# Fetching the first DFT piece over GpSimd's queue, behind a memset of half of its place

## The chip, the cores and the metric

The kernel runs on one core of a Trainium2 chip. The metric is the device time of one execution in microseconds, with all inputs and the output in the chip's memory. The kernel before was timed in three runs: median 867.17 us, lowest 867.04, highest 867.76.

## What is computed

`x` is 2048 tokens by 640 channels, in fp32. After a layer norm over the channels, two branches are added to `x`: the real part of a two-dimensional Fourier transform, written as matrix products, and an MLP that mixes the tokens.

```
x  = A_x
xn = layernorm(x)                                  # over the 640 channels
a  = xn @ dft_hid_re.T ;  b = xn @ dft_hid_im.T
A  = dft_seq_re @ a - dft_seq_im @ b               # 2048 x 2048 times 2048 x 640
u  = gelu(xn.T @ w1 + b1)                          # 640 x 1728
B  = (u @ w2 + b2).T                               # 2048 x 640
out = x + A + B
```

## The kernel before

All products are made in fp32 precision out of reduced-precision parts: an operand is cut into a high part (`high`, line 138, on ScalarE, ACT) and a low part (`low`, line 141, on VectorE, DVE), and each product is three matmuls: high by high, high by low, low by high. The kernel also saves products by sums of blocks (a Strassen-like scheme), which does not touch the place of the change. Work runs in this order: the DFT over the sequence, on columns of the DFT matrices (lines 462 to 659), the DFT over the channels, and the two products of the MLP. The instruction order of every engine is written out by hand (`manual_schedule`).

The change lies in the head, the first some 33 us. `first_columns` (line 462) makes the first 512 columns of both sequence DFT products out of the first four blocks of 128 rows of `x`. Before it, line 135 issues 13 matmuls on a constant (`WARM`), whose result is not used. The string `START` (line 44) gives the order in which the head is issued, a letter for an operation and a digit for its block:

- `x k` (line 513) loads block k of `x`, 128x640 fp32, over SP's queue. Block 0 comes as two halves of 160 KB (line 516), the others whole, 320 KB (line 518).
- `b i` (`load`, line 468) loads piece i of a DFT matrix, 128x512 fp32, 256 KB, into one of the eight places of `raw`, over SP's queue (line 470). `FIRST` (line 36) says which matrix and which block of rows; piece 0 is block 0 of the real matrix.
- `M`, `R`, `F` are the moments of a block (DVE, lines 240 and 246), the inverse root of its variance (DVE line 252, then GpSimd, called POOL in the profile, line 253), and the offset. For block 0 the offset is made by two small instructions on ACT (lines 533 and 537).
- `H` writes the high part of the normalized block (line 377 on DVE for block 0, in a part of 256 columns and one of 384; line 273 on ACT for the others), `N` normalizes the block in place (line 273, ACT), `l` and `L` write its low part (line 141, DVE).
- `T i` and `B i` cut piece i into its high part (line 138, ACT) and its low part (line 141, DVE).
- `P i` issues the matmuls of step i (line 481). The block's columns are the stationary operand, the cut piece is the moving one. The 15 of step 0 are five times high by high, five times high by low, five times low by high. Step 1 has nine, steps 2 to 4 have 15, 9 and 15.

The head's loads are issued in the order `x0 b0 x1 b1 b2 x2 b3 x3 b4 x4 x5 b5 x6 x7 b6 b7`, all on SP. GpSimd's queue carries in the head the memset of line 131, the inverse roots of line 253, and from `C` on (line 458) the stores of finished columns to `y_part`. ACT runs `T0`, the two small instructions of block 0, `N0`, `T1`, `T2` in that order; DVE runs `M0`, `R0`, `H0`, `B0`, the first half of `M1`, `l0`, `L0`, the rest of `M1`.

Of the kernel before, what the change touches and what calls it, by code (L numbers as in the profile page):

```python
# [26 lines left out]
NC = S // CH  # L27
# [13 lines left out]
FIRST_AT = [0, 1, 2, 3, 4, 5, 6, 7, 1, 3]  # L41
# [33 lines left out]
def fnet_plus_mixer(  # L75
# [30 lines left out]
    nc = tc.nc  # L106
# [30 lines left out]
    def high(hi, src):  # L137
        nc.scalar.activation(hi, src, AF.Copy)  # L138

    def low(lo, src, hi):  # L140
        nc.vector.tensor_sub(lo, src, hi.bitcast(F32))  # L141
# [76 lines left out]
    def cut_piece(source, n):  # L218

        held = {}  # L220
        j = len(steps)

        def top():
            held["piece"] = cut_place(j, n)
            high(held["piece"][:, 0, :n], source())

        def bottom():
            hi, lo = (held["piece"][:, i, :n] for i in range(2))
            low(lo, source(), hi)
            return hi, lo  # L230

        return top, bottom
# [4 lines left out]
    def half_moments(k, row, i):  # L237
        if i == 0:
            begun[k] = small.tile([P, 2, 6], F32, name="st")
        nc.vector.bn_stats(begun[k][:, i, :], row[:, i * H2 : (i + 1) * H2])  # L240

    def moments(k, row):
        for i in range(k in begun, 2):
            half_moments(k, row, i)
        st = begun[k]
        nc.vector.bn_aggr(mv[:, k, :], st.rearrange("p a b -> p (a b)"))

    def root(to, var):

        w = var.shape[-1]  # L250
        v = small.tile([P, NS], F32, name="v")[:, :w]
        (nc.vector if w <= 2 else nc.gpsimd).tensor_scalar_add(v, var, EPS)
        nc.gpsimd.tensor_tensor(to, v, power[:, :w], op=ALU.pow)

    def offset(to, ks):
        nc.vector.scalar_tensor_tensor(to[:, 1, ks], mv[:, ks, 0], -1.0, to[:, 0, ks], op0=ALU.mult, op1=ALU.mult)
# [15 lines left out]
    def normalize(k, row, by, to=None):  # L272
        nc.scalar.activation(
            row if to is None else to, row, AF.Identity, scale=by[:, 0, k : k + 1], bias=by[:, 1, k : k + 1]
        )
# [23 lines left out]
    Q = 256  # L299
# [64 lines left out]
    def first_rows(k, which, n=None):  # L364

        q, row = place_of(k)
        a = fixed[0][q]
        if row == 1 or 0 < k < 4:
            parts = [slice(0, D)]
        elif k == 0:  # L370
            parts = [slice(0, Q), slice(Q, D)]
        else:
            parts = [slice(0, Q), slice(2 * Q, D)]
        for cols in parts[n] if n else parts:
            hi, lo = (whole(a, i, row)[:, cols] for i in range(2))
            if which == 0 and k == 0:
                nc.vector.tensor_scalar(
                    hi, x_in[0][:, cols], mv[:, 0, :1], norm[:, 0, :1], op0=ALU.subtract, op1=ALU.mult
                )
            elif which == 0:  # L380
                normalize(k, x_in[k][:, cols], norm, hi)
            else:
                low(lo, x_in[k][:, cols], hi)

    def channels(k, j):

        q, row = place_of(k)
        return [whole(fixed[0][q], i, row)[:, j * P : (j + 1) * P] for i in range(2)]
# [14 lines left out]
    def later_moments(k):  # L403
        moments(k, later_pair(k % 4)[:, (k - 8) // 4, :])
# [46 lines left out]
    def c_tile():  # L451

        i = c_turn[0] = (c_turn[0] + 1) % 6
        return c_place[i // 3][:, i % 3, :]

    def store_y(h, m, c, j, t):
        if h == 0:
            nc.gpsimd.dma_start(y_part[m][c][:, j, :], t)
        else:
            nc.gpsimd.dma_start(y_part[m][c][:, j, :], t, accum_op=ALU.add)  # L460

    def first_columns():


        raw = pieces[1].rearrange("p a q c -> p (a q) c")
        banks = {}

        def load(i):
            m, k = FIRST[i][:2]
            nc.sync.dma_start(raw[:, FIRST_AT[i], :], dft_seq[m * NC, k])  # L470

        def products(w, m, k, j0, j1):

            for js in (range(j0, min(j1, 3)), range(max(j0, 3), j1)) if m else (range(j0, j1),):
                for n, (rows, cols) in enumerate(((0, 0), (0, 1), (1, 0))):
                    for j in js:
                        late = m == 1 and j >= 3
                        first, last = n == 0 and k == (2 if late else 0), n == 2 and k == (1 if late else 3)
                        if first:
                            banks[m, j] = psum[(5 * m + j) % 8]  # L480
                        nc.tensor.matmul(  # L481
                            banks[m, j], channels(k, j)[rows], w[cols], start=first, stop=last, skip_group_check=True,
                        )

        def read(m, js):
            for j in js:
                c = c_tile()
                nc.scalar.activation(c, banks[m, j], AF.Copy)
                store_y(0, m, 0, j, c)

        kept = keep.tile([P, 2, 2, CH], R32, name="kept", tag="slab6")

        def cut_kept(i, k):
            hi, lo = (kept[:, k, a, :] for a in range(2))

            def bottom():
                low(lo, raw[:, FIRST_AT[i], :], hi)
                return hi, lo

            return lambda: high(hi, raw[:, FIRST_AT[i], :]), bottom  # L500

        for i, (m, k, j0, j1) in enumerate(FIRST):
            if j0:
                piece = lambda: None, lambda k=k: (kept[:, k, 0, :], kept[:, k, 1, :])
            elif m == 1 and k < 2:
                piece = cut_kept(i, k)
            else:
                piece = cut_piece(lambda i=i: raw[:, FIRST_AT[i], :], CH)
            steps.append(piece + (lambda w, at=(m, k, j0, j1): products(w, *at),))
        for j in range(ND):  # L510
            extras[8 + j].append(lambda j=j: read(1, (j,)))

        def row(k):
            if k == 0:
                for cols in (slice(0, H2), slice(H2, D)):
                    nc.sync.dma_start(x_in[0][:, cols], x_rows[0][:, cols])  # L516
            else:
                nc.sync.dma_start(x_in[k], x_rows[k])

        def top(i):  # L520
            steps[i][0]()

        def bottom(i):
            ready[i] = steps[i][1]()

        def run(i):
            steps[i][2](ready.pop(i))

        def rooted(k, to=None):
            ks = slice(k, (to or k) + 1)  # L530
            root(norm[:, 0, ks], mv[:, ks, 1])
            if k == 0:
                nc.scalar.activation(norm[:, 1, :1], mv[:, 0, :1], AF.Copy, scale=-1.0)

        def factored(k, to=None):
            if k == 0:
                nc.scalar.activation(norm[:, 1, :1], norm[:, 1, :1], AF.Copy, scale=norm[:, 0, :1])
                return
            offset(norm, slice(k, (to or k) + 1))

        def normalized(k):
            if k < 5:
                normalize(k, x_in[k], norm)
            else:
                nc.vector.tensor_scalar(
                    x_in[k], x_in[k], mv[:, k, :1], norm[:, 0, k : k + 1], op0=ALU.subtract, op1=ALU.mult
                )

        return {
            "x": row, "b": load, "e": later_load, "T": top, "B": bottom, "P": run,  # L550
            "M": lambda k: moments(k, x_in[k]) if k < 8 else later_moments(k), "R": rooted, "F": factored,
            "H": lambda k: first_rows(k, 0), "N": normalized,
            "L": lambda k: first_rows(k, 1, slice(1, None) if k == 0 else None),
            "l": lambda k: first_rows(k, 1, slice(0, 1)), "m": lambda k: half_moments(k, x_in[k], 0), "C": lambda j, to: read(0, range(j, to + 1)),
        }
# [548 lines left out]
    with tc.manual_schedule():  # L1104
        for word in START.split():
            start[word[0]](*map(int, word[1:].split("-")))
        for i in range(8, len(steps) + 1):
# [3 lines left out]
            elif i >= s_hid:  # L1111
                k = sum(i >= s for s in (s_up, s_up + 7 * NF2, s_down))
# [44 lines left out]
```

## Time and profile before

| | |
|---|---|
| median of three runs | 867.17 us (867.04 to 867.76) |
| the profiled execution | 867.26 us, of which the span is 865.4 us |
| PE busy | 860.5 us, 99% of the span |
| DVE, ACT, POOL busy | 698.8 us (81%), 510.7 us (59%), 142.1 us (16%) |
| PE's granted clock | 9 or more tenths in all 40 slices |
| moved over SP's queue (q1) and GpSimd's queue (q0) | 95.72 MB and 50.83 MB |

A row of a timeline reads: start, time taken, engine, line, operation, tile written <- tiles read, shape, count, and in brackets the idle time before it and what ended it. Times are in us from the start of the span. PE is the matmuls, PEld the loads of stationary operands, SPq the issues of SP. A row of a chain reads: start, time taken, what. A row of DMA issues reads: tiles, issuer, operation, count, size, and the median time from issue to landing.

### The profile page before, as it was taken

The page shows a single profiled execution, that of the slowest core. Times are in us where ns is not written, and L with a number is a line of the kernel's source. Part 1 is how long each engine was busy: PE and PEld are TensorE (multiplying, and loading weights), DVE is VectorE, ACT ScalarE, POOL GpSimd, SP SyncE. Part 2 cuts the span into 40 slices and gives each one's busy share as a digit, 9 for nine tenths or more (in the row PEclk, how much of TensorE's full clock was granted, in tenths as well). Part 3 has the DMA queues.
Part 4 walks back from the last instruction along what each step waited for, and adds up shares of the span by engine and source line. Part 5 has one row for each costly group of instructions (what it writes and reads, how often), then busy time and mean ns, then how long its engine had stood idle before and what let it go on. Part 6 is the DMA issues. An engine that isn't in the chain of part 4 may idle for free.

```text
span 865.4 us, 13841 instructions
## 1 busy us (share of the span) xinstructions
PE 860.5 (99%) x4897; PEld 789.3 (91%) x4897; DVE 698.8 (81%) x1181; ACT 510.7 (59%) x928; POOL 142.1 (16%) x191
## 2 busy tenths in 40 slices
PE   9999999999999999999999999999999999999998
PEld 6888888888888888889999999999999999999998
DVE  7899888856767888677877788898779988997886
ACT  5774576543555555447565556675577765565653
POOL 2311111011021210322100101000122221111211
PEclk9999999999999999999999999999999999999999
DMA  9949254493472655779576757454567797656786
GB/s 332 358 86 341 81 193 196 136 369 49 138 142 37 194 109 150 176 120 185 113 165 177 153 138 202 157 188 142 138 156 188 173 264 170 164 133 134 154 181 132
DMA packets 86036, 147.42 MB, mean 170 GB/s; under 512 B 8496, under 2 KB 35504, under 8 KB 85712
## 3 DMA queue, kind: packets, MB, share of 16 engines
q1 hardware_dynamic: 64992, 95.72, 33.2%
q0 software_dynamic: 20976, 50.83, 31.2%
q8 instruction: 38, 0.62, 0.3%
q14 instruction: 30, 0.25, 0.1%
HBM read 99.47 MB, written 52.30 MB: 175 GB/s over the span
## 4 chain that ended last, share of the span: by engine, by line
PE 99%; DMA 0%; SPq 0%; ACT 0%; DVE 0%; issue 0%
PE psum L150 31%; PE psum L151 31%; PE psum L149 31%; PE psum L481 3%; PE psum L177 2%; DMA pieces<-in_dft_seq 0%; SPq L516 0%; ACT piece L138 0%; DVE pair L859 0%
## 5 line engine op out<-in xcount | busy, mean ns | idle before, releaser
L141 DVE TENSOR_TENSOR piece<-pieces,piece 128x512 fp32r<-128x512 f32 (+4 forms) x492 | 322.5, 659 | 122.7 <-ACT piece L138 118.4
L138 ACT ACTIVATE piece<-pieces 128x512 fp32r<-128x512 f32 (+3 forms) x468 | 292.5, 626 | 207.3 <-PE psum L151 109.5
L149 PE MATMUL psum<-piece,n 128*128 128x512 f32 x540 | 210.1, 389 | 0.0
L150 PE MATMUL psum<-piece,n 128*128 128x512 f32 x540 | 210.1, 389 | 0.0
L151 PE MATMUL psum<-piece,n 128*128 128x512 f32 x540 | 210.1, 389 | 0.0
L151 PEld LDWEIGHTS psum<-piece,n 128*128 128x128 f32 x540 | 101.4, 188 | 21.1
L149 PEld LDWEIGHTS psum<-piece,n 128*128 128x128 f32 x540 | 101.4, 188 | 21.1
L150 PEld LDWEIGHTS psum<-piece,n 128*128 128x128 f32 x540 | 101.4, 188 | 20.9
L144 DVE TENSOR_TENSOR pieces<-pieces 128x512 f32<-128x512 f32 (+3 forms) x142 | 111.9, 788 | 2.6
L149 PE MATMUL psum<-sup,piece 128*128 128x320 f32 x368 | 113.7, 309 | 0.0
L150 PE MATMUL psum<-sup,piece 128*128 128x320 f32 x368 | 113.7, 309 | 0.0
L151 PE MATMUL psum<-sup,piece 128*128 128x320 f32 x368 | 113.7, 309 | 0.0
L149 PE MATMUL psum<-sdown,piece 128*128 128x320 f32 x368 | 113.7, 309 | 0.0
L150 PE MATMUL psum<-sdown,piece 128*128 128x320 f32 x368 | 113.7, 309 | 0.0
L151 PE MATMUL psum<-sdown,piece 128*128 128x320 f32 x368 | 113.7, 309 | 0.0
L151 PE MATMUL psum<-shid,piece 128*128 128x320 f32 x280 | 86.6, 309 | 0.0
L149 PE MATMUL psum<-shid,piece 128*128 128x320 f32 x280 | 86.5, 309 | 0.0
L150 PE MATMUL psum<-shid,piece 128*128 128x320 f32 x280 | 86.5, 309 | 0.0
L863 ACT ACTIVATE pair<-psum 128x320 f32<-128x320 f32 x96 | 41.9, 436 | 57.0 <-PE psum L151 51.6
L460 POOL DMA_DIRECT2D y<-c x47 | 41.1, 938 | 185.5 <-DVE c L643 151.0
L149 PEld LDWEIGHTS psum<-sup,piece 128*128 128x128 f32 x368 | 69.1, 188 | 0.0
L150 PEld LDWEIGHTS psum<-sdown,piece 128*128 128x128 f32 x368 | 69.1, 188 | 0.0
(123 smaller groups left out, 1163.2 us busy)
## 6 DMA issues: line engine op xcount, KB each, us to landing
pieces<-in_dft_seq SPq DMA_DIRECT2D x120, 256.0 KB, 5.1
pieces<-in_w SPq DMA_DIRECT2D x88, 256.0 KB, 3.8
y<-c POOLq DMA_DIRECT2D x87, 256.0 KB, 5.6
out<-pair POOLq DMA_DIRECT2D x38, 320.0 KB, 4.8
pieces<-y SPq DMA_DIRECT2D x32, 320.0 KB, 3.7
pieces<-in_w SPq DMA_DIRECT2D x32, 192.0 KB, 3.0
out<-in_x SPq DMA_DIRECT2D x16, 320.0 KB, 8.5
pair<-in_x SPq DMA_DIRECT2D x14, 320.0 KB, 5.1
```

The costliest lines, as they stand in the source:

```text
L138: nc.scalar.activation(hi, src, AF.Copy)
L141: nc.vector.tensor_sub(lo, src, hi.bitcast(F32))
L144: nc.vector.tensor_sub(to, a, b)
L149: nc.tensor.matmul(psum, wh, mh, start=first, stop=False, skip_group_check=True)
L150: nc.tensor.matmul(psum, wh, ml, start=False, stop=False, skip_group_check=True)
L151: nc.tensor.matmul(psum, wl, mh, start=False, stop=last, skip_group_check=True)
L177: nc.tensor.matmul(psum, w, m[i], start=first and i == 0, stop=last and i == 1, skip_group_check=True)
L460: nc.gpsimd.dma_start(y_part[m][c][:, j, :], t, accum_op=ALU.add)
L481: nc.tensor.matmul(banks[m, j], channels(k, j)[rows], w[cols], start=first, stop=last, skip_group_check=True,)
L863: nc.scalar.activation(c, b, AF.Copy)
```

## The change

In `load`, piece 0 alone is treated otherwise. GpSimd first sets 256 of the 512 columns of its place to zero (`Q` is 256), and then issues the transfer on its own queue. The transfer overwrites what the memset wrote, so it waits for the memset. All other pieces stay on SP, whose list of issues becomes one shorter. No later instruction is changed.

```diff
         def load(i):
             m, k = FIRST[i][:2]
-            nc.sync.dma_start(raw[:, FIRST_AT[i], :], dft_seq[m * NC, k])
+            if i == 0:
+                nc.gpsimd.memset(raw[:, FIRST_AT[i], :Q], 0.0)
+            (nc.sync if i else nc.gpsimd).dma_start(raw[:, FIRST_AT[i], :], dft_seq[m * NC, k])
```

## Rows read from the trace of the kernel before

**Rows 1.** The page's chain of waits: shares of the span by engine.
```profile
PE 99%; DMA 0%; SPq 0%; ACT 0%; DVE 0%; issue 0%
```

**Rows 2.** The chain of waits in order of time, its head and its last piece.
```profile
0.74 0.39 SPq L516
...
1.66 3.60 DMA pieces<-in_dft_seq
5.27 0.64 ACT piece L138
5.96 27.50 PE psum L481 x120
...
862.04 0.49 DVE pair L859
```

**Rows 3.** The timeline of the head on PE, DVE and POOL.
```profile
0.79 4.41 PE L135 MATMUL psum<-const-bfloat16-1.0 128*128 128x512 bf16 x13 [0.79 <-PEq L1146]
3.08 0.89 DVE L240 BATCH_NORM_STATS2 st<-x 128x6 f32<-128x320 f32 x2 [3.08 <-DMA x<-in_x]
4.56 0.57 POOL L253 TENSOR_TENSOR norm<-v,power 128x1 f32<-128x1 f32 x1 [3.71 <-DVE v L252]
5.17 0.80 DVE L377 TENSOR_SCALAR n<-x,mv,norm 128x256 fp32r<-128x256 f32 x2 [0.76 <-POOL norm L253]
```

**Rows 4.** Instructions on tile x: line 377, duration min/median/max in ns.
```profile
L377 DVE TENSOR_SCALAR n<-x,mv,norm x2: 411/442/473, 5.2 to 5.5; 128x256 fp32r<-128x256 f32 x1, 128x384 fp32r<-128x384 f32 x1
```

**Rows 5.** The timeline of the head: what step 2's first weights wait for.
```profile
7.38 0.90 DVE L141 TENSOR_TENSOR n<-x,n 128x256 fp32r<-128x256 f32 x2 [0.34 <-ACT x L273]
10.37 0.92 ACT L273 ACTIVATE n<-x,norm 128x640 fp32r<-128x640 f32 x1 [1.78 <-DVE norm L256]
11.35 3.32 PEld L481 LDWEIGHTS psum<-piece,n 128*128 128x128 f32 x15
```

**Rows 6.** SP's issues in the timeline: piece 0 and block 1.
```profile
1.66 0.43 SPq L470 DMA_DIRECT2D pieces<-in_dft_seq  x1
2.13 0.43 SPq L518 DMA_DIRECT2D x<-in_x  x1
```

**Rows 7.** DMA issues at 1.19, 1.66 and 2.13 us, time to landing.
```profile
x<-in_x SPq DMA_DIRECT2D x1, 160.0 KB, 2.3
pieces<-in_dft_seq SPq DMA_DIRECT2D x1, 256.0 KB, 3.6
x<-in_x SPq DMA_DIRECT2D x1, 320.0 KB, 4.0
```

**Rows 8.** DMA queue from 2.0 to 3.3 us: packets, MB, share of 16 engines.
```profile
q1 hardware_dynamic: 280, 0.34, 94.9%
```

**Rows 9.** POOL's memsets: by form (busy, mean ns), and the head's in the timeline.
```profile
L806 POOL MEMSET pieces<- 128x256 f32 x2 | 1.0, 493 | 0.0
...
0.74 0.11 POOL L131 MEMSET power<- 128x16 f32 x1 [0.29 <-POOLq L1146]
```

**Rows 10.** The timeline of POOL: the first two DMA issues of the execution.
```profile
25.86 1.33 POOL L458 DMA_DIRECT2D y<-c  x2
```

**Rows 11.** Landings of POOL's issues at 99.53, 25.86 and 123.33 us, in this order.
```profile
y<-c POOLq DMA_DIRECT2D x1, 256.0 KB, 2.4
...
y<-c POOLq DMA_DIRECT2D x1, 256.0 KB, 3.8
...
y<-c POOLq DMA_DIRECT2D x1, 256.0 KB, 6.1
```

**Rows 12.** The two queues' shares, 27.2 to 28.4 us, then 28.4 to 29.2 us.
```profile
q1 hardware_dynamic: 113, 0.21, 61.8%
q0 software_dynamic: 17, 0.07, 14.1%
...
q0 software_dynamic: 60, 0.19, 60.1%
q1 hardware_dynamic: 51, 0.12, 40.0%
```

## The prediction, made before the changed kernel was run

> **What bounds the kernel now.** I read the chain of waits first, by engine and then in order of time. PE holds 99% of it [rows 1]. In order of time nothing but PE's matmuls stands in it between 5.96 us and the last eviction at 862.04 [rows 2]: once the first real matmul runs, PE doesn't stop. So what the change does to the start of that matmul goes one for one into the end, and only a new stall behind it could add to it. The 120 matmuls of the head take 27.50 us, 0.229 each [rows 2]; that is the unit for the steps below.
>
> Before 5.96 the chain is two issues on SP, then from 1.66 to 5.27 the transfer of DFT piece 0, then its high part on ACT, 0.64 [rows 2]. The reader should see that the chain enters PE through the piece and not through block 0 of `x`. Then I looked in the timeline for the second arrival, which sets how much a sooner piece can bring. The moments start at 3.08 with block 0's landing, POOL's inverse root runs from 4.56 to 5.13, and H0 from 5.17 to 5.97 [rows 3]. Its first part (256 columns) takes 0.41 and so ends at 5.58; the second ends at 5.97 [rows 4].
>
> **The change, part by part.** The sum is made against the profiled execution, 867.26 us, 0.09 above the median of 867.17; I take the 0.09 off at the end.
>
> *One issue fewer on SP.* Piece 0's issue goes from 1.66, and block 1's from 2.13 to about 1.66; the later ones follow, 0.47 sooner where SP is free [rows 6]. By itself I cost this at nothing, either way: PE waits for none of these loads. What it can do is set block 1's packets beside piece 0's.
>
> *The cap of a gain.* Were piece 0 there at once, the first matmul would wait for H0's first part, 5.58, and the usual step from writer to matmul, about 0.06 (ACT's end at 5.91 to PE at 5.96) [rows 2, 4]: 5.64. Columns 256 and up are wanted two matmuls later, at 6.10, and are there at 5.97. So the gain ends at 0.32 us. Behind it, the first weights of step 2 are loaded at 11.35, just as ACT has written them (10.37 + 0.92 = 11.29) [rows 5], while the 24 matmuls of steps 0 and 1 end at 5.96 + 24 x 0.229 = 11.46: a slack of a tenth. That path runs over `N0` on ACT, which stands behind piece 0's high part, and over DVE, which waits 0.34 for `N0` [rows 5]. So it moves with the piece by up to 0.34 either way, and a gain of 0.32 would hold; a late piece delays both paths equally and is counted once.
>
> *The memset.* POOL is free at 0.85 (0.74 + 0.11). A memset of 128x256 fp32 on POOL took 0.49 elsewhere, there over columns in four pieces; one of 16 columns took 0.11 [rows 9]. So it ends between 0.96 and 1.34, and I take the end of its own size, 1.34. The transfer waits for it, and I set the issue at 1.35. Behind the waiting transfer on POOL only the inverse roots are queued; the first is wanted at 4.56 [rows 3], and two first issues on POOL's queue took 1.33 together [rows 10], so POOL is free by 2.7 even at that sum. What covers this is block 0's landing and its moments; without that cover the memset and the issue would cost their 1.8 us or less.
>
> *The transfer on POOL's queue.* No plain load on this queue stands in the trace of before, only stores and accumulations, so I bound it by stores of the same 256 KB. In a quiet stretch one landed 2.4 us after its issue; the first of the execution, with loads on SP's queue in flight, after 3.8; one behind a long backlog on SP's queue after 6.1 [rows 11]. From 1.35 these give landings at 3.75, 5.15 and 7.45, against about 5.26 before. The nearest row is the middle one: it too is the first of its queue, and SP's queue too carries a few loads. There SP's loads had 61.8% of the engines and POOL's transfer 14.1% in the first 1.2 us; only after that did POOL's have 60.1% [rows 12].
>
> Two things speak against taking 5.15 as it stands. The 16 engines were 94.9% taken with block 0 from 2.0 to 3.3 [rows 8]; piece 0 was not waiting for its issue but for the engines, and an issue 0.3 sooner finds the same engines taken. And piece 0 itself was slow: the second half of block 0 landed at 1.19 + 2.3 = 3.49, piece 0 1.77 later, but block 1, larger by a quarter, only 0.87 after it (2.13 + 4.0 = 6.13) [rows 7]. At block 1's pace 256 KB would take 0.70, so 1.07 us go with the first reads of the DFT matrix. They go along with piece 0 to the other queue, and the store's 3.8 need not contain them. Between 0 and 1.07 more, I take 0.4, since part passes while it waits anyway: a landing at 5.55, 0.29 later than before. Then the high part and the step to PE, 0.69 as before, and PE starts at 6.25.
>
> Sum: 0.29 later at the start, no new stall behind it: 867.26 + 0.29 - 0.09 = 867.46, rounded to 867.5. Own range of this case: a landing between 5.0 and 6.2, that is -0.26 to +0.94, 866.9 to 868.1.
>
> The Trainium skill, page "DMA: Bandwidth & Descriptors", section "Issuing engines are not separate DMA queues", says that transfers from SP and GpSimd run on the same 16 engines, and that issuing from several saves only sequencer time. Rows 8 show that case: with the engines taken, the half microsecond of sequencer time saved buys no earlier bytes. Its section "Queues, rings and completion order" says that an engine goes round between queues packet by packet. By that rule POOL's transfer would start among block 0's packets; that is the second rival, and rows 12 don't agree with an even turn.
>
> **The rivals.**
> - *A real gain.* Piece 0 lands before 4.95, as the quiet row has it (3.75), and H0 is the new last arrival: -0.32, 866.9 us. For it: the issue is up to 0.7 sooner and SP's queue holds only block 0 at that time. Against: the engines are full until 3.3, and the first reads are slow.
> - *Block 0 is pushed back.* The two queues take turns, and piece 0's slow first packets go between those of the second half of block 0. The moments of that half start at once when it is there (landing 3.49, DVE at 3.53), so each delay goes into H0. PE bears 0.39 of it, since H0's second part then ends at 6.36 and is wanted two matmuls after 5.96, at 6.42 with the step. The price is at most the 1.07 of the first reads, less 0.39: +0.7, 867.9 us; the change would then do for block 0's load the opposite of what the memset in front leaves room for.
> - *POOL's transfer is starved, and the kernel is slower.* SP's issues come faster than the engines carry them, so its queue stays full, and POOL's transfer lands like the backlogged row, 6.1 after the issue, at 7.45. PE starts at 8.14, 2.18 later: 869.4 us. It counts as slower from a landing at 7.0 on. PE would have stood still from 5.2 to 8.1; if its clock fell in that gap, the price is bounded by the warm-up, whose 13 matmuls took 4.41 where 13 at 0.229 take 2.98: 1.4 more, 870.8 us. For it: 6.1 and 3.8 are rows, and SP issues 256 or 320 KB each 0.47. Against: at 1.35 only block 0 is ahead, not a backlog of microseconds.
> - *It does nothing.* Engines, not issues, set the landing, and it stays within 0.2 of 5.26: inside the forecast's own range.
>
> The Trainium skill's page "TensorE: Matmul & The Clock Gate", section "The HAM clock gate", has the slower clock return after an idle stretch of PE, which is the second price of the starved case. PE's 0.76 of idle time before 5.96 didn't bring it, as the 0.229 each of the next 120 show, and no row here has a longer gap.
>
> **How the numbers follow.** What a measurement of this kernel can tell from no change is about 0.2%, 1.73 us. The forecast (with the case that nothing changes) has 0.62, the gain 0.18, block 0 pushed back 0.10, the starved transfer 0.10. Only the last passes 1.73 us, and the cap of 0.32 leaves a faster verdict to effects I don't see: faster 0.01, same 0.89, slower 0.10. The range goes from 866.6 (the gain, less 0.3 for the scatter of runs, which were 0.7 apart) to 868.9, and leaves out the starved case.
>
> **What would show it.** In the changed profile the chain of waits should still enter PE through piece 0's high part, with its landing between 5.0 and 6.2 and PE's first matmul 0.69 later; POOL's memset should be done by 1.34; block 0's moments should start at 3.08 as before; PE should show no idle time behind its first matmul. If DVE's H0 ends after 5.97, block 0 was pushed back. If the chain enters through H0 at its old time, the gain rival holds. The prediction is wrong if piece 0 lands after 7.0, or if PE stalls again behind step 2.

## The result: slower by half a percent, past what was forecast

The changed kernel takes 871.78 us (median of six runs, 869.62 to 872.84), the kernel before 867.51 in the same session (867.04 to 867.84). Four of the changed kernel's six runs show a mean granted clock below 0.999, and they are the four above 871 us; the other two took 869.62 and 869.93. The ratio is 1.0047, with a 95% interval of 1.0036 to 1.0057. The forecast was 867.5 with a range up to 868.9, and 0.10 for slower.

The profiled execution of the changed kernel is one of its longer ones: 872.58 us, with a span of 870.5 against 865.4 before, 5.1 more. Its chain of waits in order of time, from the start to the head's last matmul, answers to [rows 2] (start, time taken, what):

```profile
0.85 0.26 POOL pieces L471
...
1.41 5.81 DMA pieces<-in_dft_seq
...
7.30 1.28 ACT L138
...
8.59 0.64 ACT piece L138
...
9.28 29.11 PE psum L483 x120
```

The chain still enters PE through piece 0, but three pieces of it are new or longer. The transfer of piece 0 ends at 7.22 and not at 5.26: 1.96 more. Behind it stands an ACT instruction of 1.28 without a tile, which was not in the chain before. PE starts at 9.28 and not at 5.96, 3.32 later, of which these two are 3.24. And the same 120 matmuls take 29.11 where they took 27.50: 1.61 more. With a wait of 0.2 on DVE in the channels' stage these make 5.1, the whole difference.

The instruction of 1.28 is the load of ACT's activation table. In the kernel before it stands near the start of the timeline (first row); in the changed kernel (the two rows below) it starts only behind the landing of piece 0, and `T0` behind it:

```profile
0.74 1.28 ACT L138 ACT_TABLE_LOAD   x1 [0.74 <-PEq L1146]
```

```profile
7.30 1.28 ACT L138 ACT_TABLE_LOAD   x1 [7.30 <-DMA pieces<-in_dft_seq]
8.59 0.63 ACT L138 ACTIVATE piece<-pieces 128x512 fp32r<-128x512 f32 x1
```

The order of ACT's first instructions in the trace shows why. Before, `T0` waited for one thing, the DMA, and carried that wait itself. Now it has two to wait for, the DMA and the memset, since both wrote the place that it reads. `T0` carries the wait for the memset; the wait for the DMA is an instruction of its own, and it stands ahead of the table load:

```
before   ACT_TABLE_LOAD, ACTIVATE piece<-pieces [waits for the DMA]
changed  wait for the DMA, ACT_TABLE_LOAD, ACTIVATE piece<-pieces [waits for the memset]
```

The longer matmuls are seen in the busy times by stretch (stretch, its length, busy time and count of PE, PEld, DVE, ACT, POOL; granted clock, DMA share, GB/s):

```profile
9.00:10.00 1.00, 0.72 (x2) 0.63 (x3) 0.75 (x2) 0.87 (x4) 0.00 (x0) 0.77 1.04 404
10.00:12.00 2.00, 2.00 (x6) 1.54 (x6) 1.65 (x4) 1.70 (x3) 0.00 (x0) 0.50 1.05 402
12.00:14.00 2.00, 2.00 (x9) 1.60 (x8) 1.49 (x6) 0.31 (x1) 0.96 (x1) 0.76 1.03 396
14.00:16.00 2.00, 2.00 (x10) 1.64 (x9) 1.83 (x6) 1.97 (x3) 0.95 (x1) 1.00 1.05 389
```

The granted clock is 0.50, the lower of PE's two levels, from some point after 9 us until some point before 14. Before that PE had stood idle for 2.90 us, against 0.76 in the kernel before. PE's waits in the whole execution are these three (what waited, for what, us in total, times, longest):

```profile
PE psum L483 <- ACT piece L138: 2.9, 1, 2.9
PE psum L135 <- PEq L1148: 0.8, 1, 0.8
PE psum L151 <- DVE piece L141: 0.2, 1, 0.2
```

The last is the one in the channels' stage, so no matmul of the head was held up by a late operand once PE had started.

### The profile page after: what moved, and what is told of

It is laid out like the page before. It is cut to its first block, busy times and chain, and to the rows that moved or that the text cites. A ratio compares the mean times of both kernels' runs of the same rounds, so it can differ in the third digit from the quotient of the medians.

```text
span 870.5 us, 13843 instructions
## 1 busy us (share of the span) xinstructions
PE 863.3 (99%) x4897; PEld 790.6 (91%) x4897; DVE 699.1 (80%) x1181; ACT 510.5 (59%) x928; POOL 142.6 (16%) x193
## 4 chain that ended last, share of the span: by engine, by line
PE 97%; DMA 1%; DVE 1%; ACT 0%; issue 0%; POOL 0%; DVEq 0%; ACTq 0%; POOLq 0%
PE psum L151 31%; PE psum L150 31%; PE psum L149 31%; PE psum L483 3%; PE psum L177 2%; DMA pieces<-y 1%; DMA pieces<-in_dft_seq 1%; DVE piece L141 0%; DVE pieces L144 0%; ACT piece L138 0%; ACT L138 0%; DVE pieces L796 0%; DVE pair L144 0%; DVE pair L861 0%; DVE sup L141 0%
```

## Where piece 0's transfer went

In the changed kernel these are the rows of the two DMA queues from 3 to 4, 4 to 5, 5 to 6 and 6 to 7.3 us (packets, MB, share of the 16 engines; q1 is SP's queue, q0 GpSimd's):

```profile
q1 hardware_dynamic: 70, 0.13, 65.8%
q0 software_dynamic: 15, 0.06, 21.0%
...
q0 software_dynamic: 48, 0.17, 63.0%
q1 hardware_dynamic: 72, 0.17, 43.9%
...
q1 hardware_dynamic: 164, 0.30, 93.2%
q0 software_dynamic: 11, 0.02, 5.3%
...
q1 hardware_dynamic: 205, 0.42, 92.6%
q0 software_dynamic: 6, 0.02, 3.1%
```

Until 5.0 us 63 of the 80 packets have been moved. The last 17 take until 7.2, while SP's later loads, issued behind piece 0, have over 90% of the engines. A load is there when its last packet is.

The trace also keeps the 16 completion counts of each transfer. Of piece 0's, 13 have come by 5.64 us (by 5.04 in the kernel before), but the last two come at 6.80 and 7.23. Those of block 1, issued behind it on SP's queue, trail too: 13 by 5.73, the last two at 7.10 and 7.55. So 0.6 of the lateness holds for the transfer as a whole, and the rest is a tail of a few counts.

## The experiments

The lateness has three candidates for causes: competition with SP's loads, the table load, and PE's clock. The table load and the clock were each taken away alone, the competition together with the table load. A run "with a lower clock" is one whose mean granted clock is below 0.999.

**The change without its memset** (`e1_no_memset`).

```diff
-            if i == 0:
-                nc.gpsimd.memset(raw[:, FIRST_AT[i], :Q], 0.0)
             (nc.sync if i else nc.gpsimd).dma_start(raw[:, FIRST_AT[i], :], dft_seq[m * NC, k])
```

> The change without its memset: piece 0 on GpSimd's queue, issued as soon as that queue is free (about 0.9 us instead of 1.41). Theory (three terms: a later landing, ACT's table load put behind the landing by the memset's second wait, and PE's clock fallen in the longer gap): the table load is back at 0.74 us, PE starts 0.69 us after the landing, and with a landing between 5.5 and 6.7 us the time is 867.4 to 868.7. Rival (the queue alone costs it all, and the table load would be hidden without trouble elsewhere): about 871, as the changed kernel. Second rival (block 0 is pushed back when the memset does not hold piece 0): the high part of block 0 on DVE starts after 5.3 instead of 5.1.

868.99 us, ratio 1.0022 (1.0012 to 1.0032). The chain in order of time, in the profiled execution (868.57 us):

```profile
1.32 5.24 DMA pieces<-in_dft_seq
...
6.58 0.64 ACT piece L138
...
7.26 27.52 PE psum L481 x120
```

The table load is back at 0.74, and PE starts 0.70 after the landing at 6.56. GpSimd issues the transfer at 1.32 and not, as I had expected, at 0.9: its memset of 0.31 delays the issue by only 0.09. H0 starts at 5.24, so block 0 is not pushed back. Four of ten runs had a lower clock and took 870.5 to 871.5. Of the other six, five lie within the forecast's 867.4 to 868.7 and one above it, at 869.27.

**The memset alone**, with piece 0 on SP as before (`e2_memset_sp`).

```diff
             if i == 0:
                 nc.gpsimd.memset(raw[:, FIRST_AT[i], :Q], 0.0)
-            (nc.sync if i else nc.gpsimd).dma_start(raw[:, FIRST_AT[i], :], dft_seq[m * NC, k])
+            nc.sync.dma_start(raw[:, FIRST_AT[i], :], dft_seq[m * NC, k])
```

> The memset alone: piece 0 stays on SP's queue in its old place, GpSimd still sets half of its place to zero first. Theory: SP's issue is not delayed (the memset ends at 1.1, the issue is at 1.66) and the landing stays near 5.26, but ACT's first instruction now waits for two things, the table load goes behind the landing, and PE starts 1.28 us later, at 7.24: 868.5 without a fall of PE's clock, up to 870.2 with it. Rival (only the queue matters): 867.4, as before.

868.69 us, ratio 1.0012 (1.0002 to 1.0022), all ten runs between 868.44 and 869.27. The chain:

```profile
1.66 3.87 DMA pieces<-in_dft_seq
...
5.60 1.28 ACT L138
6.88 0.01 issue
6.89 0.64 ACT piece L138
...
7.57 27.54 PE psum L483 x120
```

The queue is the old one, the landing nearly the old one (5.53), and the kernel is 1.2 us slower all the same. In the profile PE starts 1.61 later: 0.27 from the landing, 1.28 from the table load, the rest from the step between them. That term is shown by itself.

**The change with an early table load.** A tiny ACT instruction ahead of everything draws the table load to the front. In the first form it wrote a tile of its own (`e3_table`), in a second one with 18 matmuls for the warm-up (`e4_table_warm`).

```diff
+    tab = keep.tile([P, 1], F32, name="tab")
+    nc.scalar.activation(tab, power[:, :1], AF.Copy)
```

> The whole change, with one more tiny instruction on ACT (a copy of one column of the constant that line 131 makes) ahead of everything else, so that the table is loaded early. Theory: the landing stays near 7.2, PE starts at 7.9 instead of 9.28, and the time is 1.3 us below the changed kernel's: 870.5 where the clock falls in the gap, 869 where it does not. Rival (the table load is not on the path): 871.8 as the changed kernel.

> As the one with the early table load, and 18 instead of 13 matmuls on the constant, so that PE has no gap of more than a microsecond or two. Theory: no clock loss behind the start, the 120 matmuls of the head take 27.5 us as before instead of 29.1, and only the later landing is left: 869.2. Rival (the 1.6 us are no matter of the clock but of late operands): PE still waits, 870.5 or more.

872.53 us (1.0063) and 872.86 us (1.0060): both wrong, and for a reason outside the head. In the profile of `e3_table` PE starts at 7.30, sooner than the 7.9 I had set since the landing was sooner, and the head takes 27.54, but the span is 870.1 (one of its four runs, 875.92, had a lower clock). The counts of PE's matmuls show where the rest lies, first the kernel before, then this one (stretch, length, busy time and count, clock, DMA share, GB/s):

```profile
150.00:250.00 100.00, 100.00 (x443) 1.00 0.57 171
250.00:350.00 100.00, 100.00 (x443) 1.00 0.56 127
```

```profile
150.00:250.00 100.00, 100.00 (x439) 1.00 0.56 169
250.00:350.00 100.00, 100.00 (x435) 1.00 0.55 123
```

With PE busy throughout and the clock at 1.00, eight matmuls fewer fit into the same 100 us. The tile of 4 bytes per partition had moved the tiles that are laid out behind it. So both runs say nothing on the table load; the next two repeat them with no tile moved.

```diff
+    nc.scalar.activation(again[:, 0, :1], power[:, :1], AF.Copy)
```

> The whole change with the early table load once more, the tiny instruction now writing into a tile that is there anyway, so that no tile moves in memory. In the run with a tile of its own, PE's matmuls from 150 to 440 us came 1 to 3% slower, which had nothing to do with the head. Theory: the matmuls there are as dense as before, the table load is off the path, and 1.3 us of the change's loss are gone: landing 6.5 to 7.2, PE's start 7.2 to 7.9, 868.5 to 869.2 where PE's clock does not fall, up to 2 more where it does. Rival (the slower matmuls come from the early instruction, not from the tile's place): 872 again.

> As the one with the early table load and no tile moved, and 18 instead of 13 matmuls on the constant. Theory: PE has hardly a gap before its first real matmul, so no run loses clock: all runs between 868.0 and 869.3, no tail above 870. Rival (the tail is late operands behind the start): the tail stays.

`e5_table2`: 868.54 us, ratio 1.0016 (1.0006 to 1.0025). The matmuls are as dense as before:

```profile
250.00:350.00 100.00, 100.00 (x443) 1.00 0.56 124
```

Without the table load in the path the change's loss shrinks from 4.3 to 1.0. That is more than 1.28, since the clock also fell less often, in two of ten runs and not in four of six. Among runs that kept their clock the changed kernel took 869.62 and 869.93, this one 868.24 in the median of eight: 1.5 less. Its profiled execution (870.82 us) is one of the two of ten runs with a lower clock:

```profile
1.41 5.86 DMA pieces<-in_dft_seq
...
7.36 0.64 ACT piece L139
...
8.04 29.00 PE psum L484 x120
```

The stretch from PE's start on reads:

```profile
8.00:10.00 2.00, 1.96 (x5) 1.57 (x6) 1.64 (x4) 1.87 (x5) 0.00 (x0) 0.50 1.05 404
```

PE had been idle for 2.52 us, the granted clock from 8 to 10 us is 0.50, and the head takes 29.00; the other eight runs lie between 867.64 and 869.55. `e6_table2_warm`, with 18 warm-up matmuls, has no run with a lower clock and no tail above 870, but its median of 869.37 us (1.0021) is not lower, and six of ten runs lie above the 869.3 that I had set as the highest; in its profile PE starts at 7.64 and the head takes 27.55. That the 18 matmuls end after the high part of piece 0 in some runs would explain the median. In the profile of `e4_table_warm` they do (7.03), but only by a tenth; by how much in other runs is not shown.

**A second hardware queue** (`e7_act_queue`): piece 0 on ACT's own DMA queue, no memset.

```diff
-            nc.sync.dma_start(raw[:, FIRST_AT[i], :], dft_seq[m * NC, k])
+            (nc.sync if i else nc.scalar).dma_start(raw[:, FIRST_AT[i], :], dft_seq[m * NC, k])
```

> Piece 0 on ACT's hardware queue instead of GpSimd's, no memset, issued at 0.74 us ahead of the table load. If a second queue beside SP's is enough to make piece 0 late (the engines share their time between queues), it lands at 6 or later, as on GpSimd's queue: 868.2 or more. If it is GpSimd's way of writing its requests that makes it late, it lands near or before 5.26: 866.9 to 867.6, provided that block 0 is not pushed back (the high part of block 0 on DVE at 5.1 to 5.2).

868.34 us, ratio 1.0008 (0.9998 to 1.0017). Its queues from 2 to 3 us, and its chain:

```profile
q1 hardware_dynamic: 74, 0.09, 35.4%
q10 hardware_dynamic: 58, 0.12, 33.4%
...
1.19 3.32 DMA x<-in_x
...
6.22 0.42 DVE n L377
6.64 0.14 issue
6.78 27.44 PE psum L481 x120
```

Here piece 0 is there at about 4.1, earlier than in any other kernel, and the delay has changed sides: the second half of block 0 lands 3.3 us after its issue, where it took 2.3 [rows 7], H0 starts at 6.22, where it started at 5.17 [rows 3], and the chain enters PE through `x`. Both loads are there by 4.51, sooner than the 5.26 of before, and by 4.5 us more bytes have been moved (0.85 MB, where it was 0.69). The kernel is no faster, since the order is the wrong one: from block 0's landing to PE there are 2.27 us of moments, inverse root and H0, from piece 0's only some 0.70. The Trainium skill's page "DMA: Bandwidth & Descriptors", section "Queues, rings and completion order", has each engine go round between its queues packet by packet. For these two hardware queues the packet counts agree roughly: 74 and 58 from 2 to 3 us, 64 and 76 from 3.0 to 3.5. GpSimd's queue beside SP's had no such even turn throughout, neither in [rows 12] nor in the rows of the changed kernel above.

**SP's loads held back** (`e8_hold`): the early table load of `e5_table2`, and a memset behind GpSimd's issue that makes SP's loads from block 1 on wait for it.

```diff
             (nc.sync if i else nc.gpsimd).dma_start(raw[:, FIRST_AT[i], :], dft_seq[m * NC, k])
+            if i == 0:
+                nc.gpsimd.memset(x_in[1][:, :Q], 0.0)
```

> As the one with the early table load and no tile moved; GpSimd also sets 256 columns of block 1's place to zero, behind its issue of piece 0, so that SP's loads from block 1 on wait until about 2.5 us instead of 1.65. Theory (piece 0 is late since SP's loads are served beside and before it): with SP's queue empty behind block 0 piece 0 lands a microsecond or more sooner, 5.3 to 5.9, and the time is 867.3 to 868.0. Rival (GpSimd's queue is slow by itself, or the first reads of the matrix are): the landing stays at 6.5 to 7.2.

867.48 us, ratio 0.9999 (0.9990 to 1.0009). SP's issue of block 1 goes from 1.65 to 2.50, and the queues' shares from 3 to 4 us and the chain become:

```profile
q0 software_dynamic: 56, 0.21, 68.7%
q1 hardware_dynamic: 29, 0.03, 9.9%
...
1.41 4.06 DMA pieces<-in_dft_seq
...
6.25 27.50 PE psum L486 x120
```

Piece 0 lands at 5.47 and not at 7.2. So GpSimd's queue by itself doesn't make it that late, nor do the first reads of the matrix: it is SP's loads, issued within 0.85 us behind it. With this and the early table load the whole loss is gone, and nothing is gained either.

One landing is one execution, and landings scatter. In the eight profiles with piece 0 on GpSimd's queue and SP's loads not held back it lands between 5.81 (`e10_memset_elsewhere`) and 7.27 (`e5_table2`), so 5.47 alone would be thin evidence. What carries it is GpSimd's share from 3 to 4 us, 68.7% and not 21.0%, and the ten runs, none with a lower clock and none above 868.08. Thirteen of the 16 counts have come by 4.54 us; the last two trail here too, at 5.32 and 5.48. Why a few counts trail, and by how much in which run, no run shows.

**PE kept busy** (`e9_warm26`): the change as it is, with 26 warm-up matmuls (`WARM = 26`).

> The change as it is (table load behind the landing), with 26 instead of 13 matmuls on the constant, so that they end near 7.7 to 9.4 us and PE's gap before the first real matmul is 0 to 1.6 us instead of 2.9. Theory: the tail of runs with a lower mean clock goes; what is left is the later landing and the table load: 869.5 to 870.5, all runs within 1 us of each other, the head's 120 matmuls in 27.5 us. Rival (the matmuls behind the start are late for want of operands): 871.8 as the changed kernel, and a tail to 872.8.

870.27 us, ratio 1.0031 (1.0019 to 1.0042), all six runs between 869.95 and 870.71, none with a lower clock. The chain:

```profile
0.78 8.11 PE psum L135 x26
8.89 27.23 PE psum L483 x120
```

```profile
6.63 1.28 ACT L138 ACT_TABLE_LOAD   x1 [6.63 <-DMA pieces<-in_dft_seq]
```

PE has no gap, and the head takes 27.23 and not 29.11. The table load still stands behind the landing, which is 0.7 sooner in this profile. So the 1.61 belonged to the clock; that it was not late operands, PE's waits in the changed kernel show too.

**The memset aimed elsewhere** (`e10_memset_elsewhere`), at half of piece 7's place.

```diff
-                nc.gpsimd.memset(raw[:, FIRST_AT[i], :Q], 0.0)
+                nc.gpsimd.memset(raw[:, FIRST_AT[7], :Q], 0.0)
```

> The change with its memset aimed at half of the place of piece 7 instead of piece 0: GpSimd spends the same 0.31 us ahead of its issue, but ACT's first instruction has nothing of the memset to wait for. Theory (the table load was moved by the second wait of ACT's first instruction, and by nothing else): the table load is at 0.74 us again, the landing 6.5 to 7.2, and the time that of the kernel with the early table load, 868 to 869 with a tail to 871. Rival (any memset on GpSimd's queue ahead of the load, or the queue itself, moves it): 871.8.

870.42 us, ratio 1.0032 (1.0021 to 1.0044).

```profile
0.74 1.28 ACT L138 ACT_TABLE_LOAD   x1 [0.74 <-PEq L1148]
```

The table load stands at 0.74 again, PE starts 0.71 after the landing at 5.81 (sooner than the 6.5 to 7.2 I had set), so it is the second wait on `T0` that moves it, not a memset ahead of the issue. The median is above the forecast: four of the seven runs had a lower clock (870.4 to 872.3), the other three took 867.84 to 869.23. The gaps of those four were not seen; the profiled execution, with a gap of 1.27 us, kept its clock. Why more runs lose clock here than in `e5_table2` stays open.

## Why the prediction was wrong

*What bounds the kernel* held: the chain enters PE through piece 0, the start's delay went into the end nearly one for one, and PE didn't stop behind its first matmul but for 0.2. But the same 120 matmuls took 1.61 longer at the lower clock; the sum had no term for that, only the starved rival had.

*The memset* was costed by its time alone: 0.31 measured, inside the bounds, and the issue at 1.41 where I had set 1.35. The step that failed is the sentence that names who waits. I named what is queued behind the transfer on GpSimd, and not who reads the place: `T0` had to wait for the memset as well. And I never read ACT's first row, the table load at 0.74, whose cover was its place ahead of `T0`'s wait. Cost: 1.28 (`e2_memset_sp`), with no term for it in the sum.

*The transfer* was bounded rightly by 2.4, 3.8 and 6.1 us from issue to landing [rows 11], and the wrong row was taken. It took 5.8, near the row behind a long backlog. My reason for the middle row was that at 1.35 only block 0 is ahead. That reason fails: most packets of the loads issued next after piece 0 are served before its last ones, and SP issues one each 0.47. `e8_hold`, which delays just these, lands it at 5.47, close to my 5.55. The term was +0.29 and measured +1.96 (+0.55 to +2.01 over the eight profiles). By its own sign, a landing after 7.0, the prediction was wrong.

*The first reads* were charged with 1.07 us by a misreading of the same kind: it took the 1.77 between block 0's landing and piece 0's as piece 0's own. In that time of the kernel before SP's queue moved more than twice piece 0's 256 KB (3.5 to 5.3 us: packets, MB, share):

```profile
q1 hardware_dynamic: 284, 0.59, 90.1%
```

So piece 0 shared the engines with block 1 already there, and no run shows that the first reads cost anything.

*Issuing SP's loads sooner* I had costed at nothing, and noted that it could set block 1's packets beside piece 0's. That is where the cost came from; how much of it is due to the 0.47 sooner, and how much to the other queue, no run separates.

*The starved rival* came nearest: SP's loads made the transfer late, though mainly its last packets, and the second price for the clock, bounded at 1.4, was 1.61. I gave it 0.10 and left it out of the range. Its 869.4 and 870.8 us were below the result, since the table load was missing in both.

*Block 0 pushed back* did not happen on GpSimd's queue (H0 at 5.10; that queue had 2.7% of the engines from 2.0 to 3.3 us), but it did on ACT's, at +0.82 for PE's start. *The real gain* was not reached by any kernel: `e8_hold` is level with the kernel before. A gain at the cap of 0.32 us would be 0.04%, less than these intervals can tell.

## What to carry to other kernels

Before a tile gets a second writer, look who reads it first: a second wait of an engine's first instruction can come to stand ahead of a set-up instruction that the source doesn't show, and that instruction loses its cover. A transfer on a second queue competes with the loads that the first queue issues behind it, and either load can be the one that comes late, so hold the others back or leave the order in one queue. A gap of PE at the start is paid twice where its clock falls in it.

## What was not expected of the hardware

- With GpSimd's queue beside SP's, most of a transfer was moved early (63 of 80 packets by 5.0 us) and the last packets came 2.2 us later; between two hardware queues the packet counts were roughly even (74 and 58, then 64 and 76).
- In the two profiles with a gap of PE of 2.52 and 2.90 us the granted clock was at one half for about 3 us behind it; in those with gaps of 0.91, 1.08, 1.27 and 1.65 (`e1_no_memset`, `e2_memset_sp`, `e10_memset_elsewhere`, `e7_act_queue`) it was not.
- A tile of 4 bytes per partition, laid out ahead of the others, made PE's matmuls between 150 and 350 us up to 2% slower (443 and 435 in 100 us) and cost about 4 us (872.53 against 868.54 us). Which tile's new place does it was not tried.
